# Two leftover token tiles of an attention + mixer kernel: from four plain half products to one pair in seven half products

## The chip, the cores and the metric

The kernel runs on one core of one Trainium2 chip. The metric is device time in microseconds. Before the change, three runs took 344.31, 344.91 and 345.24 us; their median, 344.91 us, is the time that the change is held against. A core has a matrix engine (TensorE, "PE" in the profile, with its weight loads "PEld"), VectorE ("DVE"), ScalarE ("ACT"), GpSimd ("POOL") and SyncE ("SP"); SP and ACT issue DMAs here, and 16 DMA engines move the data.

## What is computed

For each of 8 lots (batch entries) with 12 heads, 448 tokens and head width 64, the reference is, cut down:

```python
scores = q @ k.T / sqrt(64) - log(448)
x = (sigmoid(scores) @ v)                  # heads side by side: 448 tokens x 768
h = relu(x.T @ w_tok1) @ w_tok2            # mixes tokens, 448 -> 256 -> 448
u = x + h.T
out = u + relu(u @ w_ch1) @ w_ch2          # mixes channels, 768 -> 1536 -> 768
```

Only the last product, `relu(u @ w_ch1) @ w_ch2`, called the output stage here, is computed in another way by the change.

## The kernel before, in words

All matmuls are in float16 with float32 sums. The order of every engine's work is written out by hand; there is no scheduler, so the order of the Python calls is the order in which each engine's queue holds its instructions. Each engine runs its own queue in order and waits where an operand, or a buffer, is not ready.

The work is cut into 24 cycles, three per lot. A cycle does the scores of four heads (line 184, with the sigmoid on ACT, line 191), the product with the values of the cycle before (`av`, line 215), a transpose through DMA (`xtrans_dma`, line 240), and the token mixing of the cycle before that (`tok1`, line 293, with a relu on ACT, line 307; then `ytrans`, line 316, whose result DVE adds into `ut`, line 323). The channel mixing of a lot follows two cycles behind: `sevens` (line 499, called at the end of a lot) computes the hidden values `h2[lot]` as seven half-size products instead of eight, with sums of operands made beforehand; the outputs leave PSUM through ACT (lines 520, 522) and DVE (lines 529, 532). `utrans` (line 334, a DMA transpose issued by SP) gives `un`, the residual with tokens on partitions. `h2` has one buffer, so the next lot's `sevens` overwrites it.

The output stage takes `h2` (1536 hidden rows x 448 tokens) times `w_ch2` (`c2`). The 448 tokens are three tiles of 128 and a rest of 64. A plain half product (`ch2`, line 549) is 12 matmuls of 128 x 384 for one tile and one half of the 768 output columns, and one DVE addition of the residual (line 572). A whole tile is two of them, 24 matmuls. The rest of 64 tokens is `last_split` (line 631) for lot 6, and `ch2_last` (lines 802 and 813, evacuated by DVE and ACT at lines 825 and 823, stored at line 834) for lot 7.

For the last two lots a second way is used: the class `ch2_seven` takes two tiles at once. Two tiles, two halves of the hidden rows and two halves of the output columns form a 2 x 2 by 2 x 2 block product, which is done as seven products of six matmuls each (`plain`, line 763), 42 matmuls for two tiles. It needs four sums of hidden blocks, made by DVE (`sums`, line 751), and four sums of weight blocks (`hsums`, made once). The seven products run in three chains, X (products 1, 6, 7, 4), Y (2) and Z (5, 3). Each chain accumulates in one PSUM bank, and after each product DVE adds the bank as it stands into the output tile (`end`, line 781), so the next product of a chain can't start before that addition has read the bank. After products 3 and 4 a tile is whole, and `store` (line 585) has SP issue two DMAs of 64 rows.

The end of the program, from the last `av` on, is a sequence of its own, outside the loop. There are eight PSUM banks: four single ones called m0 to m3 (`at_bank` names the next), and two double ones under the tag "qk". In this end part lot 6 gives tiles 0 and 1 to `ch2_seven` and tile 2 to two plain half products; then `sevens` makes `h2` of lot 7; then lot 7 does the same: tiles 0 and 1 through `ch2_seven`, tile 2 as two plain half products (lines 1318 to 1332), the rest through `ch2_last`.

The core of the class before:

```python
def sums(self, first, last):
    for n, in0, in1, op in (
        (5, lambda: self.a21, lambda: self.a22, ADD),
        (6, lambda: s[5], lambda: self.a11, SUB),
        (7, lambda: self.a11, lambda: self.a21, SUB),
        (3, lambda: self.a12, lambda: s[6], SUB),
    )[first:last]:
        ...
```

Of the kernel before, what the change touches and what calls it, by code (L numbers as in the profile page):

```python
# [9 lines left out]
FP16 = mybir.dt.float16  # L10
# [13 lines left out]
NU = 3  # L24
# [6 lines left out]
def kernel(  # L31
# [53 lines left out]
    def bank(shape, dtype, name):  # L85

        if opening_banks:
            n = opening_banks.pop(0)
        else:
            n = at_bank[0]  # L90
            at_bank[0] = (n + 1) % 4
        return pp.tile(shape, dtype, tag=f"m{n}", bufs=1, name=name)
# [146 lines left out]
    def xtrans_dma(b, u):  # L239
        nc.sync.dma_start_transpose(  # L240
            out=xn_tile(b, u).rearrange("s g t d -> s (g t) d"),
            in_=xTs[b % 2][:, u, :, :].rearrange("d g s -> d (g s)"),
        )
# [38 lines left out]
    def tok1(b, u, relu_on_vector=False, with_scores=False):  # L282

        if not with_scores:
            h1_tile(b, u)
            one = bank([128, 2, 2, 128], FP32, f"tk_{b}_{u}")
            tks[b] = [one[:, tcb, :, :] for tcb in range(2)]
        ps = tks[b]
        for tcb in range(2):
            cols = slice(128 * tcb, 128 * tcb + 128)  # L290
            for t in range(3 if with_scores else 4):
                rows = slice(0, 64 if t == 3 and N_FIRST <= NU * b + u < N_CYCLES - 2 else 128)
                nc.tensor.matmul(  # L293
                    out=ps[tcb],
                    lhsT=w1[rows, t, cols],
                    rhs=xn[b, u][rows, :, t, :],
                    start=(t == 0 and not with_scores),
                    stop=(t == (2 if with_scores else 3)),
                )
        for tcb in range(2):  # L300
            dst, src = h1[b, u][:, tcb, :, :], ps[tcb]
            if relu_on_vector:
                nc.vector.tensor_scalar(
                    out=dst, in0=src, scalar1=0.0, scalar2=None, op0=MAX
                )
            else:
                nc.scalar.activation(out=dst, in_=src, func=RELU)  # L307

    def ytrans(b, u, banks=()):
        for g in range(2):  # L310
            db = NU * g + u
            if banks:
                at_bank[0] = banks[g]
            ps = bank([128, 512], FP32, f"yt_{b}_{db}")
            for tcb in range(2):
                nc.tensor.matmul(  # L316
                    out=ps[:, 0:S],
                    lhsT=h1[b, u][:, tcb, g, :],
                    rhs=w2[:, tcb, :, :],
                    start=(tcb == 0),  # L320
                    stop=(tcb == 1),
                )
            nc.vector.tensor_tensor(  # L323
                out=uts[b % 2][:, db, 0:S], in0=xTs[b % 2][:, u, g, 0:S], in1=ps[:, 0:S], op=ADD
            )


    def utrans(b):
        if b < B - 1:
            nc.vector.tensor_copy(  # L330
                out=uts[b % 2][:, 0:NU, S:512], in_=uts[b % 2][:, NU:NDB, S - 64 : S]
            )
        un[b] = pa.tile([128, NDB, 4, 128], FP16, tag="un", bufs=2, name=f"un_{b}")
        nc.sync.dma_start_transpose(
            out=un[b].rearrange("s db t d -> s (db t) d"),
            in_=uts[b % 2].rearrange("d db s -> d (db s)"),
        )
# [203 lines left out]
    def ch2(b, t, half, n0=0, n1=NCB):  # L541
        cols = slice(DH * half, DH * half + DH)
        if n0 == 0:
            if half == 0:
                outs[b, t] = pa.tile([128, D], FP32, tag="outs", bufs=3, name=f"o_{b}_{t}")
            acc[b] = bank([128, 512], FP32, f"c2_{b}_{t}_{half}")
        ps = acc[b]
        for cb in range(n0, n1):
            nc.tensor.matmul(  # L549
                out=ps[:, 0:DH],  # L550
                lhsT=h2[b][:, BY_GROUP[cb], 128 * t : 128 * t + 128],
                rhs=c2[:, BY_GROUP[cb], cols],
                start=(cb == 0),
                stop=(cb == NCB - 1 and b in un),
            )
        if n1 < NCB:
            return
        if b not in un:
            for n in range(NU):
                nc.tensor.matmul(  # L560
                    out=ps[:, 128 * n : 128 * n + 128],
                    lhsT=uts[b % 2][:, NU * half + n, 128 * t : 128 * t + 128],
                    rhs=ident[:, :],
                    start=False,
                    stop=(n == NU - 1),
                )
        ch2_out(b, t, half, ps)
# [147 lines left out]
    class ch2_seven:  # L715

        CHAIN = {1: "X", 6: "X", 7: "X", 4: "X", 2: "Y", 5: "Z", 3: "Z"}

        def __init__(self, b, X, Y, Z):
            self.b, self.ps, self.banks = b, {}, {"X": X, "Y": Y, "Z": Z}  # L720
            hid = pa.tile(
                [128, 3, NCB // 2, 128], FP16, tag="tr_k", bufs=2, name=f"hid_{b}"
            )
            hid3 = pa.tile([128, NCB // 2, 128], FP16, tag="tr_q", bufs=2, name=f"hid3_{b}")
            self.held = {n: hid[:, at, :, :] for at, n in enumerate((5, 6, 7))}
            self.held[3] = hid3[:, :, :]
            h = h2[b]
            t0, t1 = slice(0, 128), slice(128, 256)
            self.a11, self.a12 = h[:, LOW, t0], h[:, HIGH, t0]
            self.a21, self.a22 = h[:, LOW, t1], h[:, HIGH, t1]  # L730
            self.weights = {1: self.a11, 2: self.a12, 4: self.a22}
            self.moving = {
                1: c2[:, LOW, D1],
                2: c2[:, HIGH, D1],
                3: c2[:, HIGH, D2],
                5: hsums[0],
                6: hsums[1],
                7: hsums[2],
                4: hsums[3],
            }  # L740
# [12 lines left out]
        def begin(self, n):  # L753
            chain = self.CHAIN[n]
            if n in (1, 2, 5):
                at_bank[0] = self.banks[chain]
                self.ps[chain] = bank([128, 512], FP32, f"c8_{self.b}_{n}")
            return self.ps[chain]

        def plain(self, n, k0=0, k1=NCB // 2):  # L760
# [11 lines left out]
                self.end(n)  # L772

        def end(self, n):
            b = self.b
            t, half = {1: (0, 0), 2: (0, 0), 6: (0, 1), 3: (0, 1)}.get(n, (1, int(n != 4)))
            if (b, t) not in outs:
                outs[b, t] = pa.tile([128, D], FP32, tag="outs", bufs=3, name=f"o_{b}_{t}")
            o = outs[b, t][:, DH * half : DH * half + DH].rearrange("s (u d) -> s u d", d=128)
            opens = n in (1, 6, 5, 4)  # L780
            nc.vector.tensor_tensor(
                out=o,
                in0=un[b][:, NU * half : NU * half + NU, t, :] if opens else o,
                in1=self.ps[self.CHAIN[n]][:, 0:DH].rearrange("s (u d) -> s u d", d=128),
                op=ADD,
            )
            if n in (3, 4):
                store(b, t)
# [485 lines left out]

    lot = B - 2
    before, ahead = divmod(N_CYCLES - 1, NU), divmod(N_CYCLES - 2, NU)
    seven = ch2_seven(lot, X, X + 1, X + 1)
    av(*before, banks=two_banks("xa_end"))
    steps, last_end = last_split(lot, two_banks("c2_end"))
    for f in steps:  # L1280
        f()
    seven.sums(0, 2)

    def halves(b, t, half):
        return [lambda n=n: ch2(b, t, half, n, n + 6) for n in (0, 6)]

    first, second = halves(lot, 2, 0), halves(lot, 2, 1)
    xtrans_dma(*before)
    seven.plain(1)
    seven.plain(2)  # L1290
    seven.sums(2, 4)
    seven.plain(6)
    seven.plain(5)
    last_end()
    at_bank[0] = Y
    tok1(*ahead)
    seven.plain(7)
    seven.plain(3)
    at_bank[0] = Y
    ytrans(*ahead)  # L1300
    token_sums(B - 1, 0, 2)
    seven.plain(4)
    at_bank[0] = X + 1
    first[0]()
    at_bank[0] = Y
    tok1(*before)
    first[1]()
    at_bank[0] = Y
    ytrans(*before)
    at_bank[0] = X  # L1310
    second[0]()
    second[1]()
    token_sums(B - 1, 2, NU)
    utrans(B - 1)
    sevens(B - 1)
    seven = ch2_seven(B - 1, Y + 1, Y, X)
    first, second = halves(B - 1, 2, 0), halves(B - 1, 2, 1)
    seven.plain(1)
    seven.sums(0, 4)
    seven.plain(2)  # L1320
    at_bank[0] = X + 1
    for f in first:
        f()
    seven.plain(5)
    seven.plain(6)
    at_bank[0] = Y
    second[0]()
    seven.plain(3)
    seven.plain(7)
    second[1]()  # L1330
    seven.plain(4)
    at_bank[0] = X
    for w, f in pieces_last(B - 1):
        f()

# [29 lines left out]
```

## Time and profile before

| | value |
|---|---|
| runs | 344.31, 344.91, 345.24 us; median 344.91 us |
| the profiled execution's own time | 343.85 us |
| its span (first to last instruction) | 341.9 us |
| granted TensorE clock | 1.00 |
| busy: PE / PEld / DVE / ACT / POOL | 334.7 / 238.8 / 216.7 / 212.5 / 56.6 us |
| product of six 128 x 384 matmuls, start to start | 0.98 us |
| DVE addition of a 128 x 384 bank (lines 781, 572) | 0.55 to 0.56 us |
| DVE sum of hidden blocks, 128 x 768 f16 (line 751) | 0.49 to 0.56 us |
| ACT copy out of PSUM, 128 x 896 / 128 x 448 (lines 520, 522) | 0.92 / 0.54 us |
| lot 7's `sevens`, start | 312.36 us |
| lot 7's output stage, start / `ch2_last`, start | 324.43 / 335.25 us |
| the last two stores issued (ACT, SP) | 338.14 and 338.17 us |

Times in the trace are counted from the start of the span. "L763" is line 763 of the kernel before. A line of the timeline gives the start, the length, the engine, the line, the operation, what it writes and reads, and the number of instructions merged; in brackets stands the idle time before it and what ended it. "c" is any PSUM bank of the output stage, "hid" a sum of hidden blocks, "h" is `h2`, "o" an output tile, "hsum" a sum of weight blocks. A line of windows gives, for a stretch of time, each engine's busy time, the granted clock, the mean busy share of the DMA engines and the rate at which they moved data. SPq and ACTq are DMA-issuing instructions.

### The profile page before, as it was taken

How to read it: one execution, taken by the hardware profiler on the slowest of the kernel's cores; microseconds unless marked ns; L12 is line 12 of the kernel's file. 1: busy time of each engine (PE TensorE's matmuls, PEld its weight loads, DVE VectorE, ACT ScalarE, POOL GpSimd, SP SyncE). 2: the span in 40 equal slices, each digit the busy share in tenths (PEclk: the TensorE clock that was granted, in tenths of full speed). 3: DMA queues.
4: the chain of work that ended last, by engine and by line, in shares of the span. 5: the costliest groups of instructions: out<-in, count | busy, mean ns of one | idle time of the engine just before them, and what ended most of it. 6: DMA issues, size and time to landing. Idle time of an engine off the chain costs nothing.

```text
span 341.9 us, 10439 instructions
## 1 busy us (share of the span) xinstructions
PE 334.7 (98%) x4549; PEld 238.8 (70%) x4549; DVE 216.7 (63%) x438; ACT 212.5 (62%) x271; POOL 56.6 (17%) x98
## 2 busy tenths in 40 slices
PE   7999999999999999999999999999999999999994
PEld 4655566555886679766886679766896669768952
DVE  3376467588674775566574584666765685886662
ACT  4996846588658684877648785777648885102400
POOL 8992440040040004000130004000100000000000
PEclk9999999999999999999999999999999999999999
DMA  7999999999999799999999599948991438035406
GB/s 125 172 180 191 207 204 200 169 175 223 219 172 208 119 175 175 209 168 134 191 188 167 123 196 184 223 98 149 199 157 33 102 78 141 5 69 130 86 0 161
DMA packets 104380, 52.17 MB, mean 153 GB/s; under 512 B 76432, under 2 KB 101264, under 8 KB 104336
## 3 DMA queue, kind: packets, MB, share of 16 engines
q1 hardware_dynamic: 78944, 29.70, 47.8%
q0 software_dynamic: 25168, 21.50, 41.7%
q8 instruction: 35, 0.57, 0.7%
q10 hardware_dynamic: 224, 0.33, 0.3%
q14 instruction: 9, 0.07, 0.1%
HBM read 43.45 MB, written 11.01 MB: 159 GB/s over the span
## 4 chain that ended last, share of the span: by engine, by line
PE 90%; ACT 5%; DMA 1%; DVE 1%; issue 1%; ACTq 0%; DVEq 0%
PE c_ab L499 14%; PE qk L184 10%; PE c L549 9%; PE c_c L499 8%; PE c L375 8%; PE xa L215 8%; PE c L631 6%; PE tk L293 5%; PE yt L316 5%; ACT att L191 5%; PE c L763 4%; PE c L613 4%; PE c L352 3%; DMA first_q<-in_q_dram 1%; PE c L802 1%; PE c_a L499 1%
## 5 line engine op out<-in xcount | busy, mean ns | idle before, releaser
L191 ACT ACTIVATE att<-qk,att_bias 128x896 f16<-128x896 f32 x168 | 157.0, 1015 | 41.5 <-PE qk L184 41.1
L184 PE MATMUL qk<-tr_q,tr_k 64*64 64x448 f16 x672 | 57.5, 356 | 0.5 <-DVE tr_k L176 0.2
L499 PEld LDWEIGHTS <-c 128*128 128x128 f16 x504 | 48.4, 98 | 1.1 <-issue 0.3
L224 DVE CAST xT<-xa 128x448 f16<-128x448 f32 x46 | 26.6, 620 | 29.8 <-PE xa L215 29.8
L215 PE MATMUL xa<-att,raw_v 64*64 64x448 f16 x644 | 38.0, 349 | 0.0
L499 PEld LDWEIGHTS <-sum 128*128 128x128 f16 x378 | 36.3, 98 | 0.0
L184 PEld LDWEIGHTS <-tr_k 64*64 64x64 f16 x672 | 20.3, 105 | 19.7 <-issue 12.0
L572 DVE TENSOR_TENSOR o<-un,c 128x384 f32<-128x384 f16 x34 | 18.8, 554 | 23.3 <-PE c L613 10.2
L549 PE MATMUL c<-c,h 128*128 128x384 f16 x180 | 32.9, 326 | 0.0
L375 PE MATMUL c<-c,h 64*64 64x384 f16 x640 | 31.1, 322 | 0.0
L520 ACT ACTIVATE pt_ab<-c_ab 128x896 f32<-128x896 f32 x21 | 19.3, 917 | 16.9 <-PE c_ab L499 16.3
L323 DVE TENSOR_TENSOR ut<-xT,yt 128x448 f16<-128x448 f16 x48 | 27.5, 614 | 1.9 <-PE yt L316 1.9
L215 PEld LDWEIGHTS <-raw_v 64*64 64x64 f16 x672 | 20.3, 107 | 10.9 <-issue 0.4
L1039 POOL COPY gate<-tr_q 128x2 f16<-128x2 f16 x6 | 1.2, 195 | 154.0 <-DMA tr_q<-rel_q 154.0
L549 PEld LDWEIGHTS <-h 128*128 128x128 f16 x180 | 17.2, 98 | 11.3 <-issue 1.0
L307 ACT ACTIVATE h<-tk 128x256 f16<-128x256 f32 x42 | 14.2, 405 | 16.7 <-PE tk L293 16.7
L375 PEld LDWEIGHTS <-h 64*64 64x64 f16 x640 | 18.7, 107 | 7.9
L316 PE MATMUL yt<-w,h 128*128 128x448 f16 x96 | 22.1, 353 | 0.0
L631 PE MATMUL c<-c,h 64*64 64x384 f16 x480 | 22.1, 322 | 0.0
L522 ACT ACTIVATE h<-c_ab 128x896 f16<-128x896 f32 x7 | 6.4, 917 | 24.4 <-PE c_ab L499 24.4
L293 PE MATMUL tk<-xn,w 128*128 128x256 f16 x156 | 21.2, 274 | 0.1
L529 DVE TENSOR_TENSOR h<-pt_ab,c_ab 128x896 f16<-128x896 f32 x14 | 15.2, 1084 | 9.4 <-PE c_ab L499 9.4
(110 smaller groups left out, 473.3 us busy)
## 6 DMA issues: line engine op xcount, KB each, us to landing
out_dram<-o SPq DMA_DIRECT2D x48, 192.0 KB, 3.5
c<-in_moe_w_ch_dram POOLq DMA_DIRECT2D x4, 1152.0 KB, 15.6
raw_k<-in_k_dram POOLq DMA_DIRECT2D x10, 336.0 KB, 9.3
raw_q<-in_q_dram POOLq DMA_DIRECT2D x10, 336.0 KB, 13.3
raw_v<-in_v_dram POOLq DMA_DIRECT2D x10, 336.0 KB, 10.8
out_dram<-o SPq DMA_DIRECT2D x15, 96.0 KB, 2.2
raw_q<-in_q_dram POOLq DMA_DIRECT2D x12, 112.0 KB, 4.9
raw_k<-in_k_dram POOLq DMA_DIRECT2D x12, 112.0 KB, 4.8
```

The costliest lines, as they stand in the source:

```text
L184: nc.tensor.matmul(out=ps[64 * g : 64 * g + 64, hi, 0:S], lhsT=tr[b, "k"][64 * hi : 64 * hi + 64, u, j, 64 * g : 64 * g + 64], rhs=tr[b, " ...
L191: nc.scalar.activation(out=att[b, u, j][:, :, :], in_=ps[:, :, 0:S], func=SIGMOID, bias=bias_t[:, :], scale=att_scale,)
L215: nc.tensor.matmul(out=ps[g][64 * hi : 64 * hi + 64, 0:S], lhsT=raw[b, "v"][64 * g : 64 * g + 64, u, hi, j, :], rhs=att[b, u, j][64 * g : ...
L224: nc.vector.tensor_copy(out=xTs[b % 2][:, u, g, 0:S], in_=ps[g][:, 0:S])
L293: nc.tensor.matmul(out=ps[tcb], lhsT=w1[rows, t, cols], rhs=xn[b, u][rows, :, t, :], start=(t == 0 and not with_scores), stop=(t == (2 if ...
L316: nc.tensor.matmul(out=ps[:, 0:S], lhsT=h1[b, u][:, tcb, g, :], rhs=w2[:, tcb, :, :], start=(tcb == 0), stop=(tcb == 1),)
L323: nc.vector.tensor_tensor(out=uts[b % 2][:, db, 0:S], in0=xTs[b % 2][:, u, g, 0:S], in1=ps[:, 0:S], op=ADD)
L375: nc.tensor.matmul(out=ps[p][m : m + 64, 0:n], lhsT=lhsT(p, part, m), rhs=rhs(p, part), start=(first and turn == 0), stop=(last and turn = ...
L499: nc.tensor.matmul(out=ps[:, g, p, :], lhsT=weights[n][:, d, 128 * cb : 128 * cb + 128], rhs=moving[n][:, d, :], start=(n in (1, 5, 2) and ...
L520: nc.scalar.activation(out=shaped(part[:, :, :]), in_=ps, func=COPYF)
L549: nc.tensor.matmul(out=ps[:, 0:DH], lhsT=h2[b][:, BY_GROUP[cb], 128 * t : 128 * t + 128], rhs=c2[:, BY_GROUP[cb], cols], start=(cb == 0), ...
L631: nc.tensor.matmul(out=ps[r][m : m + 64, 0:DH], lhsT=lhsT(part, n, m), rhs=rhs(part, n, m), start=(n == 0), stop=(n == n_cb - 1),)
```

## The change

Tile 2 of lot 6 and tile 2 of lot 7 are now a pair of their own, and go through `ch2_seven` together after lot 7's `sevens`. Since `h2` is overwritten by then, ACT first copies lot 6's tile 2 (12 blocks of 128 tokens) to a tile `held`, in a buffer that the values of lot 6 have left. The output tile of lot 7's tile 2 takes another such buffer. The class gets the two rows of output and the two sides of hidden values as arguments. The order of the end is dealt anew: the token mixing and `utrans` of lot 7 stand earlier, between the products of lot 6's pair, `ytrans` writes to the double banks, `token_sums` is done in one piece instead of two, and the products of the two pairs of the last part alternate.

```diff
-    def ytrans(b, u, banks=()):
+    def ytrans(b, u, banks=None):
...
-            ps = bank([128, 512], FP32, f"yt_{b}_{db}")
+            ps = banks[g] if banks else bank([128, 512], FP32, f"yt_{b}_{db}")
...
-        def __init__(self, b, X, Y, Z):
+        def __init__(self, rows, sides, X, Y, Z):
...
+            (self.a11, self.a12), (self.a21, self.a22) = [
+                (side[:, LOW, :], side[:, HIGH, :]) for side in sides
+            ]
...
+    held = pa.tile([128, NCB, 128], FP16, tag="raw_v", bufs=2, name="held")
+    nc.scalar.activation(out=held[:, :, :], in_=tokens(h2[lot], 2), func=COPYF)
     seven.sums(0, 2)
-    first, second = halves(lot, 2, 0), halves(lot, 2, 1)
     xtrans_dma(*before)
+    last_end()
     seven.plain(1)
     seven.plain(2)
     seven.sums(2, 4)
-    seven.plain(6)
-    seven.plain(5)
-    last_end()
     at_bank[0] = Y
     tok1(*ahead)
+    seven.plain(6)
+    at_bank[0] = Y + 1
+    tok1(*before)
+    ytrans(*ahead, banks=two_banks("yt_end_1"))
+    seven.plain(5)
+    ytrans(*before, banks=two_banks("yt_end_2"))
+    utrans(B - 1)
     seven.plain(7)
+    token_sums(B - 1)
     seven.plain(3)
-    at_bank[0] = Y
-    ytrans(*ahead)
-    token_sums(B - 1, 0, 2)
     seven.plain(4)
-    first[0]()
-    tok1(*before)
-    first[1]()
-    ytrans(*before)
-    second[0]()
-    second[1]()
-    token_sums(B - 1, 2, NU)
-    utrans(B - 1)
     sevens(B - 1)
-    seven = ch2_seven(B - 1, Y + 1, Y, X)
-    first, second = halves(B - 1, 2, 0), halves(B - 1, 2, 1)
+    outs[B - 1, 2] = pa.tile([128, D], FP32, tag="raw_v", bufs=2, name=f"o_{B - 1}_2")
+    both = ch2_seven([(lot, 2), (B - 1, 2)], [held, tokens(h2[B - 1], 2)], Y, Y + 1, Y + 1)
+    seven = ch2_seven([(B - 1, 0), (B - 1, 1)], [...], X + 1, X, X)
+    both.plain(1)
+    seven.sums(0, 2)
+    both.plain(2)
     seven.plain(1)
-    seven.sums(0, 4)
     seven.plain(2)
-    for f in first:
-        f()
-    seven.plain(5)
+    both.sums(0, 2)
     seven.plain(6)
-    second[0]()
-    seven.plain(3)
+    seven.plain(5)
+    seven.sums(2, 4)
+    both.plain(6)
+    both.plain(5)
+    both.sums(2, 4)
     seven.plain(7)
-    second[1]()
+    seven.plain(3)
+    both.plain(7)
+    both.plain(3)
     seven.plain(4)
-    at_bank[0] = X
+    both.plain(4)
+    at_bank[0] = Y + 1
     for w, f in pieces_last(B - 1):
         f()
```

More of the change, by code (lines that the diff above doesn't have):

```diff
@@ L307, in tok1 @@
                 nc.scalar.activation(out=dst, in_=src, func=RELU)
-    def ytrans(b, u, banks=()):
+    def ytrans(b, u, banks=None):
         for g in range(2):
             db = NU * g + u
-            if banks:
-                at_bank[0] = banks[g]
-            ps = bank([128, 512], FP32, f"yt_{b}_{db}")
+            ps = banks[g] if banks else bank([128, 512], FP32, f"yt_{b}_{db}")
             for tcb in range(2):
@@ L717 @@
         CHAIN = {1: "X", 6: "X", 7: "X", 4: "X", 2: "Y", 5: "Z", 3: "Z"}
-        def __init__(self, b, X, Y, Z):
-            self.b, self.ps, self.banks = b, {}, {"X": X, "Y": Y, "Z": Z}
+        def __init__(self, rows, sides, X, Y, Z):
+            self.rows, self.ps, self.banks = rows, {}, {"X": X, "Y": Y, "Z": Z}
+            b = rows[1][0]
             hid = pa.tile(
@@ L726, in __init__ @@
             self.held[3] = hid3[:, :, :]
[L727 to L730, printed above, removed]
+            (self.a11, self.a12), (self.a21, self.a22) = [
+                (side[:, LOW, :], side[:, HIGH, :]) for side in sides
+            ]
             self.weights = {1: self.a11, 2: self.a12, 4: self.a22}
@@ L756, in begin @@
                 at_bank[0] = self.banks[chain]
-                self.ps[chain] = bank([128, 512], FP32, f"c8_{self.b}_{n}")
+                b, t = self.rows[1]
+                self.ps[chain] = bank([128, 512], FP32, f"c8_{b}_{t}_{n}")
             return self.ps[chain]
@@ L774, in end @@
         def end(self, n):
-            b = self.b
-            t, half = {1: (0, 0), 2: (0, 0), 6: (0, 1), 3: (0, 1)}.get(n, (1, int(n != 4)))
+            row, half = {1: (0, 0), 2: (0, 0), 6: (0, 1), 3: (0, 1)}.get(n, (1, int(n != 4)))
+            b, t = self.rows[row]
             if (b, t) not in outs:
@@ L1276, with tokens @@
     before, ahead = divmod(N_CYCLES - 1, NU), divmod(N_CYCLES - 2, NU)
-    seven = ch2_seven(lot, X, X + 1, X + 1)
+    def tokens(side, t):
+        return side[:, :, 128 * t : 128 * t + 128]
+    seven = ch2_seven(
+        [(lot, 0), (lot, 1)], [tokens(h2[lot], t) for t in range(2)], X, X + 1, X + 1
+    )
     av(*before, banks=two_banks("xa_end"))
@@ L1281 @@
         f()
+    held = pa.tile([128, NCB, 128], FP16, tag="raw_v", bufs=2, name="held")
+    nc.scalar.activation(out=held[:, :, :], in_=tokens(h2[lot], 2), func=COPYF)
     seven.sums(0, 2)
-    def halves(b, t, half):
-        return [lambda n=n: ch2(b, t, half, n, n + 6) for n in (0, 6)]
-    first, second = halves(lot, 2, 0), halves(lot, 2, 1)
     xtrans_dma(*before)
+    last_end()
     seven.plain(1)
@@ L1291 @@
     seven.sums(2, 4)
+    at_bank[0] = Y
+    tok1(*ahead)
+    seven.plain(6)
[5 more added lines that the diff above has]
+    utrans(B - 1)
+    seven.plain(7)
+    token_sums(B - 1)
+    seven.plain(3)
+    seven.plain(4)
+    sevens(B - 1)
+    outs[B - 1, 2] = pa.tile([128, D], FP32, tag="raw_v", bufs=2, name=f"o_{B - 1}_2")
+    both = ch2_seven(
+        [(lot, 2), (B - 1, 2)], [held, tokens(h2[B - 1], 2)], Y, Y + 1, Y + 1
+    )
+    seven = ch2_seven(
+        [(B - 1, 0), (B - 1, 1)], [tokens(h2[B - 1], t) for t in range(2)], X + 1, X, X
+    )
+    both.plain(1)
+    seven.sums(0, 2)
+    both.plain(2)
+    seven.plain(1)
+    seven.plain(2)
+    both.sums(0, 2)
     seven.plain(6)
     seven.plain(5)
-    last_end()
-    at_bank[0] = Y
-    tok1(*ahead)
+    seven.sums(2, 4)
+    both.plain(6)
+    both.plain(5)
+    both.sums(2, 4)
     seven.plain(7)
     seven.plain(3)
-    at_bank[0] = Y
-    ytrans(*ahead)
-    token_sums(B - 1, 0, 2)
+    both.plain(7)
+    both.plain(3)
     seven.plain(4)
-    at_bank[0] = X + 1
-    first[0]()
-    at_bank[0] = Y
-    tok1(*before)
-    first[1]()
-    at_bank[0] = Y
-    ytrans(*before)
-    at_bank[0] = X
-    second[0]()
-    second[1]()
-    token_sums(B - 1, 2, NU)
-    utrans(B - 1)
-    sevens(B - 1)
-    seven = ch2_seven(B - 1, Y + 1, Y, X)
-    first, second = halves(B - 1, 2, 0), halves(B - 1, 2, 1)
-    seven.plain(1)
-    seven.sums(0, 4)
-    seven.plain(2)
-    at_bank[0] = X + 1
-    for f in first:
-        f()
-    seven.plain(5)
-    seven.plain(6)
-    at_bank[0] = Y
-    second[0]()
-    seven.plain(3)
-    seven.plain(7)
-    second[1]()
-    seven.plain(4)
-    at_bank[0] = X
+    both.plain(4)
+    at_bank[0] = Y + 1
     for w, f in pieces_last(B - 1):
```

## The prediction

> **What bounds the kernel now.** I read the page's busy shares first, then the chain that ended last, then the end part alone: windows, the PE, DVE and SP timelines, and the DMA landings.
>
> ```profile
> PE 334.7 (98%) x4549; PEld 238.8 (70%) x4549; DVE 216.7 (63%) x438; ACT 212.5 (62%) x271; POOL 56.6 (17%) x98
> ...
> PE 90%; ACT 5%; DMA 1%; DVE 1%; issue 1%; ACTq 0%; DVEq 0%
> ```
>
> The reader is to see that 90% of the chain is PE. An average may hide a stage, so here are the windows of the output stage of lot 7:
>
> ```profile
> 325.00:330.00 5.00, 5.00 (x33) 2.99 (x32) 4.22 (x9) 0.17 (x1) 0.00 (x0) 1.00 0.00 0
> 330.00:335.00 5.00, 5.00 (x33) 2.99 (x31) 2.28 (x5) 0.00 (x0) 0.00 (x0) 1.00 0.18 37
> ```
>
> PE is busy 5.00 us of 5, at a clock of 1.00; DVE (third pair of numbers) is busy 4.22 us of 5 in the first half and is the engine to watch. The PE timeline gives the price of a product:
>
> ```profile
> 298.36 2.12 PE L763 MATMUL c<-c,h 128*128 128x384 f16 x12
> 300.32 2.11 PE L763 MATMUL c<-hsum,hid 128*128 128x384 f16 x12
> 302.27 1.04 PE L293 MATMUL tk<-xn,w 128*128 128x256 f16 x8
> 303.14 1.14 PE L763 MATMUL c<-hsum,hid 128*128 128x384 f16 x6
> ...
> 312.36 1.31 PE L499 MATMUL c_ab<-ut,c 128*128 128x224 f16 x12
> ...
> 324.43 2.11 PE L763 MATMUL c<-c,h 128*128 128x384 f16 x12
> ...
> 335.25 2.14 PE L802 MATMUL c<-c,h 128*64 128x384 f16 x24
> ```
>
> A length includes the tail of the last matmul, so I count from start to start: two products take 300.32 - 298.36 = 1.96 us, one 0.977, one matmul 0.163. No bracket with idle time stands on any PE line from 294 us on: matmuls removed there shorten the path one for one, as long as nothing else becomes late.
>
> **The change, part by part.**
>
> *Products.* Before, each tile 2 is two half products of 12 matmuls, 48 for both lots. After, the pair is 7 x 6 = 42. Six matmuls go: 6 x 0.163 = **0.98 us** off PE. Ahead of lot 7's `sevens` 24 matmuls leave (3.90 us), so it starts at 312.36 - 3.90 = 308.46; behind it 18 are added: 84 matmuls in place of 324.43 to 335.25's 66. Everything up to the end part is the same list of instructions.
>
> *The copy `held`.* ACT does 128 x 1536. No row has it; 0.54 us for 448 columns and 0.92 for 896 give 0.84 ns a column, so 1.46 us (between 0.92, the nearest row, and twice my value). It runs from 295.0, when `h2` is whole; ACT idles there for 8.5 us until 303.34, its next work comes at about 301.3, and `h2` is overwritten only after 308. Cost nothing; without that idle time it would delay the relu and then `ytrans` by its own length.
>
> *The token mixing, moved ahead.* The order is now products 1, 2, `tok1`, 6, `tok1` of the last cycle, `ytrans`, 5, `ytrans`, 7, 3, 4. The tightest need is the transposed xn for the second `tok1`: SP issues it at 297.82 as before, it landed 3.05 us later (300.87), and PE now wants it at 298.36 + 3 x 0.98 + 0.87 = 302.2 instead of 307.8. Slack 1.3 us: no cost. `last_end`'s additions come earlier on DVE, at 298.7, and delay product 1's addition from 299.55 to about 299.7 to 300.3; product 6 needs it at 301.2. SP's queue now has `last_end`'s stores and then `utrans` (about 306.7 instead of 314.3); the two stores of lot 6's pair wait behind its 4.3 us of issue, and nothing reads them. `token_sums` ends on DVE at 309.2, the first product that reads it comes at 311.3. Product 4 needs product 7's addition by 307.5; it ends at 307.27, the same 0.22 us of slack that product 6 had behind product 1 before (300.10 to 300.32), without a stall.
>
> *DVE in the last stage.* Before, the stage had 7 + 2 additions and 4 sums. After: 14 additions and 8 sums, 22 instructions in 13.7 us of PE. What one costs:
>
> ```profile
> 325.61 0.56 DVE L781 TENSOR_TENSOR o<-un,c 128x384 f32<-128x384 f16 x1 [0.31 <-PE c L763]
> 326.08 0.55 DVE L751 TENSOR_TENSOR hid<-h 128x768 f16<-128x768 f16 x1
> 326.66 0.56 DVE L751 TENSOR_TENSOR hid<-hid,h 128x768 f16<-128x768 f16 x1
> 327.14 0.55 DVE L751 TENSOR_TENSOR hid<-h 128x768 f16<-128x768 f16 x1
> ```
>
> Starts are 0.47 us apart, 0.58 where the second reads the first's result, and an addition starts 0.20 us after its product's last matmul was due to pass (325.41 to 325.61). I laid the new order out with these three numbers, keeping 324.43 as the stage's start. The pair's products 1 and 2 read `held` and cover the time in which `h2` is finished. Three places are tight. Product 6 of tiles 0 and 1 is due at 328.34; the addition before it in its bank ends at 328.16. Product 5 is due at 329.31; its bank is free at 329.09. Product 6 of the pair is due at 330.29; the sum that it loads as weights ends at 330.15 (it waits behind the addition of product 2 of tiles 0 and 1, 328.54). In the opening a weight load follows DVE by 0.10 us (xT copied by 29.39, load at 29.49), and the load itself takes 0.10: matmul at 330.35, a **stall of 0.06**. Bounds: 0 with no such delay, 0.30 if each instruction takes its full 0.56 and the delay is 0.20. All later needs have 0.2 us or more.
>
> *Stores at the end.* Four tiles leave in place of three in the last microseconds: tiles 0 of lot 7, 2 of lot 6, 1 and 2 of lot 7, the last three 0.98 us apart.
>
> ```profile
> 333.01 4.35 SPq L585 DMA_DIRECT2D out_dram<-o  x6
> ...
> 338.14 0.54 ACTq L834 DMA_DIRECT2D out_dram<-o  x1
> 338.17 0.47 SPq L834 DMA_DIRECT2D out_dram<-o  x1
> ```
>
> A tile takes SP two issues, 1.2 us. So three tiles ready at 333.0, 334.0 and 335.0 (before's clock less the 3.9 us) are issued until 336.7; the last store, due 0.92 us earlier than 338.17, at 337.25, finds SP free. The six landings before came 2.60, 2.70, 2.64, 2.75, 2.95 and 2.84 us after issue: two tiles in a row add 0.2 us, a third about 0.1 more. Before, the last pair of stores landed at 340.33 (SP, 2.16 us) and 340.56 (ACT, 2.42 us), 0.7 and 1.0 us behind the last tile's 339.60; now they come 0.3 us closer behind it. I take **0.10 us** lost, between 0 and 0.7 (the second rival).
>
> *The very end.* After the last landing SP steps through its final waits, a semaphore pair each:
>
> ```profile
> L1360 SPq EVENT_SEMAPHORE  x8: 27/28/28, 340.6 to 341.0; - x8
> L1360 SPq DRAIN  x1: 13/13/13, 341.1 to 341.1; - x1
> ```
>
> It waits for the eight DMA semaphores in a fixed order, 0.06 us a step. In before's instruction list ACT's last store, the latest to land (340.56), counts on the first of them, so eight steps follow it, 0.5 us to the drain at 341.07. In the changed list ACT's store has the last of the eight and SP's the third. SP's lands at 340.33 - 0.92 + 0.10 = 339.51; five steps later it is 339.82, ACT's has landed at 339.74, and the drain stands at about 339.90 instead of 341.07.
>
> *Sum.* PE's end: -0.98 + 0.06 = -0.92. Landing: +0.10. Final waits: 0.35 less. Together **-1.17 us**: a span of 341.9 - 1.2 = 340.7. The profiled execution took 343.85 us with a span of 341.9, so 1.95 lie around it; the median of the runs is 1.06 above it. I put the difference on the median: 344.91 - 1.17 = **343.75 us**, 0.34% less.
>
> **The rivals.**
>
> 1. *DVE becomes the bound of the last stage.* For: 22 instructions in 13.7 us, one each 0.62. Against: starts 0.47 to 0.58 apart in the same mix. At 0.60 apart PE would lose 0.7 us (344.4), at 0.65 1.5 us (345.2).
>
> 2. *The stores bunch up.* From the first data of lot 6's tile 2 to the end, three tiles and the last store are 1.38 MB. Two tiles in a row moved 0.79 MB from 336.0 to 339.3, 238 GB/s: 5.8 us from 334.3, to 340.1, where the forecast needs 339.4. That loses 0.7 us: 344.4. Against: the landings followed the issues by nearly the same time, so issue set that rate; at the 310 GB/s of 337 to 338 us nothing is lost. The Trainium skill ("Trainium Kernel Development and Optimization", Key Constraints) says that stores issued by SP and ACT run on the same 16 DMA engines and interleave, which speaks against the change: ACT's last store has no way past SP's tiles. The trace agrees in kind, 2.42 us on ACT beside 2.16 on SP. By its "Perfetto Trace Analysis" (Roofline), about 435 GB/s for one core, 1.38 MB would take an estimated 3.2 us and nothing would be lost.
>
> 3. *Slower: xn comes late.* The second `tok1` now reads xn 4.4 us after its transpose is issued, instead of 10. From a landing time of 4.4 us on PE waits one for one; from 5.6 us the kernel is slower than before. Lengths of 6.4 us (the median for tr_q) would cost 2.0 us: 345.8; the longest of this transpose was 11.3. Against: the last four took 3.0 to 3.2 us, with the DMA engines idle, as they are here (share 0.00 from 296 to 298 us).
>
> 4. *The end does not shorten*: the final waits cost what they did, because ACT's store lands well behind the rest, or the step order plays no part. -0.82 us: 344.1.
>
> **How the numbers follow.** Forecast 0.60, its own range 343.2 to 344.2 (stall 0 to 0.3, landing 0 to 0.3, and 0.4 us for the scatter of the runs). DVE bound 0.10, stores 0.10, xn late 0.05, end not shorter 0.12; 0.03 for a slowdown I have no row for. The range that holds 8 in 10 reaches down to 343.1 and up to **344.7**, over the second and fourth rival and the milder half of the first. 0.3% is 1.03 us, about what a measurement of this kernel can tell from no change, so faster means below 343.87. My forecast lies just beyond: of its 0.60 I give 0.50 to faster, with 0.05 from the others: 0.55. Slower (above 345.9) is half of the third rival, the far part of the first and the 0.03: 0.08. The rest, 0.37, is within 0.3%.
>
> **What would show it.** Lot 7's `sevens` starts at 308.5 in the new trace; `ch2_last` at about 334.3; PE has no idle bracket from 294 us on, or one of about 0.1 us at the pair's product 6. Then xn lands about 3 us after 297.8, and the copy `held` takes about 1.5 us on ACT ahead of 301. The last store is issued at 337.2, lands at 339.5 to 339.8, and the drain follows within 0.15 us of ACT's landing. Wrong would be: idle time of PE behind DVE in the last stage, the last store's landing over 2.7 us, or a `tok1` that waits for xn.

## The result, and the profile after

Over 21 runs of each kernel the median went from 344.93 to 345.9 us; the ratio is 1.0036 (95% interval 1.0019 to 1.0052). The change made the kernel slower by about a third of a per cent, where the prediction had 343.75 us and 343.1 to 344.7 as its range. The profiled execution of the changed kernel took 345.8 us with a span of 344.0, at a granted clock of 1.00.

Of the changed kernel's page, the busy shares and the chain that ended last by engine:

```profile
PE 335.3 (97%) x4543; PEld 238.7 (69%) x4543; DVE 219.6 (64%) x441; ACT 214.3 (62%) x272; POOL 56.7 (16%) x98
...
PE 90%; ACT 5%; DVE 2%; DMA 1%; issue 1%; ACTq 0%; DVEq 0%
```

PE has the six matmuls less (4543 for 4549), and still its busy time is 0.6 us longer and the chain gives DVE 2% where it gave 1%. By the windows of both traces the longer busy time lies ahead of lot 6's pair (296.76 us up to its first product, 295.46 before), where PE has the same instructions in both kernels; behind it PE is busy 38.55 us, 39.20 before. The last section treats that. What DVE has to do with the end shows in the chain from 303 us on. Its columns are start, length, and what was running:

```profile
304.40 0.39 PE yt_end L314 x2
...
304.81 0.63 DVE ut L321
...
305.49 0.54 PE yt_end L314 x2
...
307.04 0.56 DVE o L780
307.59 0.54 DVE ut L321
...
308.17 0.54 PE yt_end L314 x2
...
323.71 13.65 PE c L762 x84
```

Twice the chain leaves PE for DVE in the middle of a `ytrans`: two matmuls, an addition on DVE, then the other two matmuls. The PE timeline of the same stretch says how long PE stood still:

```profile
304.23 0.54 PE L314 MATMUL yt_end<-w,h 128*128 128x448 f16 x2
305.49 0.54 PE L314 MATMUL yt_end<-w,h 128*128 128x448 f16 x2 [0.71 <-DVE ut L321]
305.86 1.14 PE L762 MATMUL c<-hsum,hid 128*128 128x384 f16 x6
306.84 0.54 PE L314 MATMUL yt_end<-w,h 128*128 128x448 f16 x2
308.17 0.54 PE L314 MATMUL yt_end<-w,h 128*128 128x448 f16 x2 [0.80 <-DVE ut L321]
308.55 1.14 PE L762 MATMUL c<-hsum,hid 128*128 128x384 f16 x6
...
311.47 1.31 PE L497 MATMUL c_ab<-ut,c 128*128 128x224 f16 x12
...
323.55 2.11 PE L762 MATMUL c<-c,held 128*128 128x384 f16 x12
...
337.29 2.14 PE L801 MATMUL c<-c,h 128*64 128x384 f16 x24
```

The two brackets are waits that the prediction does not have. From start to start the two halves of a `ytrans` are 1.26 us (305.49 - 304.23) and 1.33 us (308.17 - 306.84) apart; without a wait they are 0.38 (two matmuls of 448 columns, as e1 below shows). 1.26 + 1.33 - 2 x 0.38 = **1.83 us** lost. The 84 matmuls of the last stage, from 323.71 on, have no gap.

**One clock for two traces.** Up to product 1 of lot 6's pair (298.36 us before, 299.55 after) PE has the same instructions in both kernels, yet the after trace is 1.19 us late there. That belongs to the execution (the last section shows from what). So I measure all kernels from this product's start, which takes the scatter of the opening out: to lot 7's `sevens`, to `ch2_last`, and to the end of the span.

| kernel | `sevens` | `ch2_last` | end | last two stores, issue to landing (ACT / SP) | last landing to end | median, us | ratio to before [95%] |
|---|---|---|---|---|---|---|---|
| before | 14.00 | 36.89 | 43.55 | 2.42 / 2.16 | 1.35 | 344.93 | |
| after | 11.92 | 37.74 | 44.48 | 2.79 / 2.59 | 1.05 | 345.9 | 1.0036 [1.0019, 1.0052] |
| e1_own_tiles | 10.09 | 35.91 | 42.66 | 2.83 / 2.62 | 1.03 | 344.31 | 0.9978 [0.9960, 0.9997] |
| e2_pair_early | 10.10 | 35.91 | 42.68 | 2.52 / 2.27 | 1.35 | 343.92 | 0.9954 [0.9941, 0.9968] |
| e3_pair_alone | 11.00 | 36.93 | 43.68 | 2.82 / 2.62 | 1.03 | 345.0 | 0.9993 [0.9976, 1.0010] |
| e4_one_store_less | 10.10 | 35.91 | 42.33 | 2.42 / 2.15 | 1.11 | 343.51 | 0.9949 [0.9921, 0.9978] |
| e5_stores_on_two_queues | 10.09 | 35.91 | 42.50 | 2.42 / 2.15 | 1.28 | 344.04 | 0.9995 [0.9967, 1.0023] |
| e6_products_then_adds | 10.09 | 35.91 | 42.65 | 2.81 / 2.61 | 1.05 | 344.01 | 0.9973 [0.9951, 0.9994] |
| e7_reorder_alone | 14.00 | 36.89 | 43.60 | 2.47 / 2.20 | 1.35 | 344.73 | 1.0009 [0.9992, 1.0025] |
| e8_last_wait_last | 10.09 | 35.91 | 42.32 | 2.41 / 2.14 | 1.11 | 343.68 | 0.9968 [0.9949, 0.9986] |

The kernel before, run beside e1 to e4, had a median of 345.14; beside e5 to e8, 345.05.

From this mark the change costs 44.48 - 43.55 = +0.93 us; the medians differ by 0.97. Its parts: products -0.98 (24 matmuls less ahead of `sevens`, -3.90, and 18 more behind it, 25.82 us from `sevens` to `ch2_last` in place of 22.89: +2.93; a rounding of 0.01), the waits in `ytrans` +1.83, the landing of ACT's last store +0.37, the final waits -0.30. Together +0.92.

### The profile page after: what moved, and what is told of

Its sections match the earlier page's. It is cut to its first block, busy times and chain, and to the rows that moved or that the text cites. A ratio compares the mean times of both kernels' runs of the same rounds, so it can differ in the third digit from the quotient of the medians.

```text
span 344.0 us, 10437 instructions
## 1 busy us (share of the span) xinstructions
PE 335.3 (97%) x4543; PEld 238.7 (69%) x4543; DVE 219.6 (64%) x441; ACT 214.3 (62%) x272; POOL 56.7 (16%) x98
## 4 chain that ended last, share of the span: by engine, by line
PE 90%; ACT 5%; DVE 2%; DMA 1%; issue 1%; ACTq 0%; DVEq 0%
PE c_ab L497 14%; PE qk L184 10%; PE c_c L497 8%; PE c L373 8%; PE xa L215 8%; PE c L547 6%; PE c L762 6%; PE c L629 6%; PE tk L293 5%; PE yt L314 5%; ACT att L191 5%; PE c L611 4%; PE c L350 3%; DMA first_q<-in_q_dram 1%; PE c L801 1%; PE c_a L497 1%
## 5 line engine op out<-in xcount | busy, mean ns | idle before, releaser
L570 DVE TENSOR_TENSOR o<-un,c 128x384 f32<-128x384 f16 x30 | 16.6, 554 | 20.7 <-PE c L611 10.2
L321 DVE TENSOR_TENSOR ut<-xT,yt 128x448 f16<-128x448 f16 x44 | 25.2, 615 | 1.9 <-PE yt L314 1.9
L373 PEld LDWEIGHTS <-h 64*64 64x64 f16 x640 | 18.7, 107 | 7.9
L547 PE MATMUL c<-c,h 128*128 128x384 f16 x132 | 24.1, 326 | 0.0
L527 DVE TENSOR_TENSOR h<-pt_c,c_c 128x448 f16<-128x448 f32 x21 | 13.0, 617 | 12.3 <-PE c_c L497 12.3
L314 PE MATMUL yt<-w,h 128*128 128x448 f16 x88 | 20.3, 353 | 0.0
L629 PEld LDWEIGHTS <-h 64*64 64x64 f16 x528 | 15.4, 107 | 6.7
```

The lines of the kernel that those rows point to most:

```text
L314: nc.tensor.matmul(out=ps[:, 0:S], lhsT=h1[b, u][:, tcb, g, :], rhs=w2[:, tcb, :, :], start=(tcb == 0), stop=(tcb == 1),)
L321: nc.vector.tensor_tensor(out=uts[b % 2][:, db, 0:S], in0=xTs[b % 2][:, u, g, 0:S], in1=ps[:, 0:S], op=ADD)
L373: nc.tensor.matmul(out=ps[p][m : m + 64, 0:n], lhsT=lhsT(p, part, m), rhs=rhs(p, part), start=(first and turn == 0), stop=(last and turn = ...
L527: nc.vector.tensor_tensor(out=shaped(dst), in0=shaped(parts[gs, which]), in1=ps, op=ADD)
L547: nc.tensor.matmul(out=ps[:, 0:DH], lhsT=h2[b][:, BY_GROUP[cb], 128 * t : 128 * t + 128], rhs=c2[:, BY_GROUP[cb], cols], start=(cb == 0), ...
L629: nc.tensor.matmul(out=ps[r][m : m + 64, 0:DH], lhsT=lhsT(part, n, m), rhs=rhs(part, n, m), start=(n == 0), stop=(n == n_cb - 1),)
```

## The experiments

My theory after the result: `ytrans` gets both halves of a double bank as one tile. The code writes half 0, has DVE add it, writes half 1, has DVE add that. Waits are kept by tile, so the second product waits until the first addition has read the tile, though it writes another bank. The changed kernel's instruction list for PE has that wait (a row is the number, the line, the instruction, and what it waits for):

```
8564 L314 Matmult yt_end_5994<-w_69,h_7_2_5966 128x448
...
8568 L314 Matmult yt_end_5994<-w_69,h_7_2_5966 128x448 [waits DVE_49]
```

The rivals were that the token mixing's relu comes late in the new order, and that the loss is only the opening's scatter. The second is out by the table: the loss stands behind the mark, +0.93 us, and the medians of 21 runs each agree with it.

**e1_own_tiles**: each product gets a tile, and with it a double bank, of its own.

```diff
-    ytrans(*ahead, banks=two_banks("yt_end_1"))
+    ytrans(*ahead, banks=[two_banks(f"yt_end_1{g}")[0] for g in range(2)])
(yt_end_2 likewise)
```

> The changed kernel, with each of the four ytrans products of the last lot in a double bank of its own (its first half used) instead of two products sharing one double bank as one tile. Theory T (one tile, one wait): the second product of each pair waits until DVE has read the first, because both lie in one tile; in the trace of the changed kernel this is 1.26 us from start to start instead of 0.38, and 1.33 instead of 0.38, together 1.83 us. T expects both gaps at 0.38, sevens of lot 7 starting 10.1 us after product 1 of lot 6's pair (11.92 in the changed kernel, 14.0 in the kernel before), and a time 1.8 us below the changed kernel, near 344.1 us, 0.25% below the kernel before. Rival R1 (the relu is late: tok1 now stands close ahead of ytrans): the gaps stay, 345.9 us. Rival R2 (the loss is the 1.19 us by which the opening of the profiled execution was longer, all else is even): no change, 345.9 us, with the opening 1.2 us longer than in the kernel before.

PE's timeline of e1:

```profile
305.76 0.92 PE L314 MATMUL yt_end<-w,h 128*128 128x448 f16 x4
306.52 1.14 PE L762 MATMUL c<-hsum,hid 128*128 128x384 f16 x6
307.50 0.92 PE L314 MATMUL yt_end<-w,h 128*128 128x448 f16 x4
```

Both brackets are gone: four matmuls in 0.76 us (306.52 - 305.76), and the end comes 44.48 - 42.66 = 1.82 us sooner, the 1.83 of the two waits. With that alone the change pays, if narrowly: 0.9978, with an interval that ends at 0.9997.

**e6_products_then_adds**: the tile stays shared; in `ytrans` both products are written before the two additions.

```diff
-            nc.vector.tensor_tensor(out=uts[b % 2][:, db, 0:S], ..., in1=ps[:, 0:S], op=ADD)
+            adds.append(add)        # add holds this same addition
+            if not banks:
+                adds.pop()()
+        for add in adds:
+            add()
```

> The changed kernel with its shared double banks kept, but in each ytrans both products are written first and DVE's two additions come after them, as av does with its two banks. Theory T: the second product then has no reader ahead of it in its tile, PE does not wait, sevens of lot 7 starts 10.1 us after product 1 of lot 6's pair, time as e1, near 344.2 us. R1 (late relu): 11.9 us and 345.9 us.

PE's timeline of e6 at the two `ytrans`, and DVE's at the first:

```profile
304.82 0.92 PE L315 MATMUL yt_end<-w,h 128*128 128x448 f16 x4
...
306.55 0.92 PE L315 MATMUL yt_end<-w,h 128*128 128x448 f16 x4
```

```profile
305.77 1.15 DVE L324 TENSOR_TENSOR ut<-xT,yt_end 128x448 f16<-128x448 f16 x2 [1.07 <-PE yt_end L315]
```

Same tile, same banks, no wait on PE: the order of writers and readers was what cost the time. DVE shows the tile as the unit from the other side. Its first addition starts 0.95 us after the products' start, 0.2 after all four matmuls (304.82 + 0.76). In e1, with a tile each, it starts at 306.34, 0.58 after 305.76, 0.2 after the first two (0.38). The chip itself does not ask for it: by the Trainium skill ("PSUM — Partial Sum Buffer", section "PSUM bank collisions raise a hardware error") two engines must be kept apart on one bank, and these are two banks. The runs agree so far as e1, in which the products have no order to the other's addition, takes the full 1.82 us back.

**e3_pair_alone**: the pair in the last part as in after, but the order ahead of lot 7's `sevens` as before.

```diff
+    last_end(); tok1(*ahead)      # behind product 5, ahead of 7
+    ytrans(*ahead)                # behind product 3, single banks
+    tok1(*before); ytrans(*before); utrans(B - 1)   # behind product 4
```

> The pair in seven products alone: tok1, ytrans, token_sums and utrans of lot 7 stay where they were in the kernel before, in single banks; only the plain half products of lot 6's tile 2 that stood between them are gone. Theory T: no wait on a shared tile, but the relu of the second tok1 has nothing to hide behind: PE idles about 0.95 us ahead of the second ytrans and about 0.2 at the start of sevens. Time: 344.9 - 0.98 + 1.15 + 0.4 (stores) - 0.3 (final waits) = 345.2 us, 0.7 below the changed kernel. R1 and R2: no better than the changed kernel, 345.9 or above.

PE's timeline of e3, ahead of `sevens`:

```profile
309.97 0.92 PE L314 MATMUL yt<-w,h 128*128 128x448 f16 x4 [0.75 <-ACT h L307]
310.72 1.42 PE L497 MATMUL c_ab<-ut,c 128*128 128x224 f16 x12
```

This is what the first rival looks like: PE waits 0.75 us for the relu (ACT, line 307), because the plain halves of tile 2 that covered it are gone. `sevens` starts 0.91 later than in e1, and the last store still lands late. From the mark the end is 43.68, 0.13 behind before; timed, 0.9993. So by the traces the pair needs the reordered front to gain anything (43.68 here, 42.66 in e1; the intervals of the timed ratios overlap), and e1 and e6, which have it, show no wait for the relu at all. The rival falls for after.

**e7_reorder_alone**: e1's front, but without `held` and the second pair; tile 2 of both lots in plain halves as before.

```diff
-    held = pa.tile([128, NCB, 128], FP16, tag="raw_v", bufs=2, name="held")
-    nc.scalar.activation(out=held[:, :, :], in_=tokens(h2[lot], 2), func=COPYF)
...
+    for f in halves(lot, 2, 0) + halves(lot, 2, 1):
+        f()
```

> The new order of the token mixing alone, with own tiles for ytrans as in e1, but without the pair: tile 2 of lot 6 and of lot 7 go through plain half products as in the kernel before (lot 6's four groups stand together ahead of sevens). As many matmuls as before, no wait: sevens 14.0 us after product 1, the span's end 43.55 us after it, time that of the kernel before, 344.9 to 345.2 us, ratio 1.000. If the new order itself cost something that the pair hides, it shows here as idle time of PE.

Every mark is that of before within 0.05 us, and the ratio is 1.0009. Moving the token mixing costs nothing and brings nothing by itself.

**e4_one_store_less**: e1 without the store of lot 6's tile 2.

```diff
-            if n in (3, 4):
+            if n in (3, 4) and (b, t) != (B - 2, 2):
                 store(b, t)
```

> e1_own_tiles without the two DMAs that store lot 6's tile 2 (that tile of the output is left unwritten). T: with one tile less in the last microseconds the last two stores land 2.4 us (ACT) and 2.2 us (SP) after issue, as in the kernel before; in this list ACT's store has the seventh of the eight final waits, SP's the first. Time 0.4 us below e1, near 343.7 us. If it is not the number of stores that delays the last ones, the lags stay at 2.6 to 2.8 us and the time at that of e1.

The time from issue to landing of the last two stores (SP, ACT), after and e4:

```profile
DMA to landing us min/median/max: 2.6/2.7/2.8
```

```profile
DMA to landing us min/median/max: 2.1/2.3/2.4
```

One tile less in front of them, and they are as quick as before the change; the end comes 0.33 us sooner than in e1. So the stores in front are what makes them late. It need not be the number of tiles: e4 also has two tiles in a row where after has three (1.20 and 1.28 us apart), and its last tile store is issued 1.37 us ahead of ACT's last store, after's 1.07. In e2 below all four tiles are stored, but in rows of two and with the same 1.37 us, and most of the delay is gone. The runs do not separate the row from that distance. In after the eight tile stores land 2.61, 2.71, 2.62, 2.73, 2.98, 2.94, 2.94 and 3.06 us after their issue.

**e2_pair_early**: e1, with the last stage dealt so that the pair's tiles leave earlier and further apart; the sums move along with their products.

```diff
-    (1, 2 of both; 1, 2 of seven; 6, 5, 6, 5, 7, 3, 7, 3, 4, 4 alternating)
+    both 1, 2; seven 1, 2; both 6, 5, 7, 3; seven 6; both 4; seven 5, 7, 3, 4
```

> e1_own_tiles, and in the last stage the products of the pair of tiles 2 are drawn ahead, so that the tiles are whole 1.95, 2.9 and 0.98 us apart instead of three of them 0.98 us apart, as many products as before. Theory T adds that three tiles stored 0.98 us apart hold up the last two stores (2.79 us on ACT and 2.59 on SP after issue in the changed kernel, 2.42 and 2.16 before): here they should fall back to about 2.4 and 2.2, 0.4 us less. In this kernel's list ACT's last store counts on the first of the eight DMA semaphores that SP waits for at the end, as in the kernel before, so about 0.35 us after the last landing come back: together 344.0 us, as e1 or 0.1 below. If the stores are not held up by each other, the lags stay at 2.6 to 2.8 and the time is 0.35 above e1.

The stores do land sooner (2.52 and 2.27), but the span ends as in e1: ACT's store, the last to land, now counts on the first of the eight final waits, so 1.35 us follow it, not 1.03. The gain of 0.31 in landing was given back there. Its timed ratio, 0.9954 from five runs, is better than the trace accounts for (-0.87 us, or 0.9975).

**e5_stores_on_two_queues**: e2, with the second half of each of the last tiles issued by ACT.

```diff
-            nc.sync.dma_start(
+            queue = nc.scalar if par == 1 and (b == B - 1 or (b, t) == (B - 2, 2)) else nc.sync
+            queue.dma_start(
```

> e2_pair_early, and the second half of each of the last four tiles is issued by ACT instead of SP. The stores stand in time 0.6 us less behind each other at issue. T: the last two stores land 2.4 (ACT) and 2.2 us (SP) after issue as in the kernel before (2.52 and 2.27 in e2): from the start of product 1 of lot 6's pair to the end 42.6 us (42.68 in e2), time 0.1 below e2, near 343.8 us. ACT's last store counts on the second of the eight final waits. If ACT's issues get in the way of its last copy, the last store is issued later than SP's by over 0.3 us and the time is above e2.

The last stores land as in e4, with all tiles stored, and the span ends 0.16 us sooner than e1's. The timed ratio, 0.9995 with an interval 0.56% wide, cannot tell that: three of twelve runs were above 346 us.

**e8_last_wait_last**: e5, and two earlier stores go through GpSimd's queue, so that ACT's last store counts on the last of the final waits.

```diff
+            if (b, t) == (B - 2, 0):
+                queue = nc.gpsimd
```

> e5_stores_on_two_queues, and the two DMAs of lot 6's tile 0, some 25 us before the end, are issued by GpSimd. They are off every path; what they change is the count of DMAs, so that ACT's last store counts on the eighth and SP's on the first of the eight semaphores that SP waits for at the end. If the order of the final waits is worth what the traces show (1.35 us from the last landing to the end of the span where ACT's store counts on the first, 1.05 where it counts on the last), the time is 0.3 us below e5, near 343.5 us, and 1.05 us lie between the last landing and the end. If the order plays no part, both are as in e5, with 1.3 us.

1.11 us follow the last landing instead of 1.28: 0.18 us less at the end, not 0.3, because in e5 the store had come to stand on the second wait. It is not 1.05 either: SP's last store now counts on the first wait and lands at 340.42, and the steps run on from 340.43 to 340.89, so that the last of them finds ACT's store, landed at 340.65, already there. In e4, with SP's store on the first wait and ACT's on the seventh, 1.11 us follow as well. By the trace e8 ends 1.23 us ahead of before; timed it is 0.9968. Of the versions tried it has the shortest end with all stores in place, and it is faster than both kernels; e2's and e8's intervals overlap, so the runs do not tell which of the two is the faster.

## Why the prediction was wrong, point by point

- *Products*: right. Without the waits `sevens` comes 3.91 us sooner (10.09 for 14.00; forecast 3.90), and the 18 matmuls behind it cost 2.93.
- *The copy `held`*: right. It took 1.48 us (estimate 1.46), from 296.20, in ACT's idle time.
- *The token mixing, moved ahead, "no cost"*: **this step failed, by 1.83 us.** It followed each operand (xn landed 3.04 us after its issue, 1.3 us ahead of its use, as forecast; the relu was in time) and each chain's bank, but of `ytrans` only its place. That both its products now lie in one tile, with a DVE addition between them in the code, was in the diff (`banks[g]` from one `two_banks`). Before, each product took a tile of its own from m0 and m1. The second wait is longer than the first because DVE does product 5's addition (307.04) first and only then the addition that PE waits for (307.51), as DVE's timeline of after shows. The 0.03 that I gave to "a slowdown I have no row for" was the place of this case, and 0.08 for slower was too little.

```profile
307.04 0.56 DVE L780 TENSOR_TENSOR o<-un,c 128x384 f32<-128x384 f16 x1 [0.35 <-PE c L762]
307.51 0.61 DVE L321 TENSOR_TENSOR ut<-xT,yt_end 128x448 f16<-128x448 f16 x1
```

- *DVE in the last stage*: no stall, where I had 0.06. At the pair's product 6, its sum ended at 329.26, when it was due by the forecast (330.15 on before's clock, less 0.88), but the weight load followed at 329.32, 0.05 us later where I had taken 0.10, and the matmul started in its turn at 329.40. DVE's share in that stage, after:

```profile
325.00:330.00 5.00, 5.00 (x33) 3.02 (x31) 4.55 (x10) 0.00 (x0) 0.00 (x0) 1.00 0.00 0
330.00:335.00 5.00, 5.00 (x33) 3.01 (x31) 4.58 (x10) 0.00 (x0) 0.00 (x0) 1.00 0.00 0
```

  DVE is busy 4.55 and 4.58 us of 5, PE all 5.00. The first rival falls, with little room. How 0.60 and 0.65 us for one instruction come to 0.7 and 1.5 us the prediction does not show (22 x 0.60 = 13.2 us is less than the stage's 13.7), and no run tests these two prices.
- *Stores at the end*: the mechanism was right, the term mis-sized: +0.37 for 0.10, within its bounds of 0 to 0.7. I read the lags of two tiles in a row and added 0.1 for a third; the last two stores lost 0.37 and 0.43. The second rival is thus half true, as e4 and e2 show.
- *The very end*: right. After the last landing 1.05 us follow, 1.35 before: -0.30 for -0.35. Five steps are left behind SP's landing at 342.80, with ACT's at 342.98. The final waits of after:

```profile
L1362 SPq EVENT_SEMAPHORE  x5: 28/28/28, 342.9 to 343.1; - x5
L1362 SPq DRAIN  x2: 7/10/13, 343.2 to 343.3; - x2
```

- *Third rival, xn late*: fell; no `tok1` waits. *Fourth rival*: fell; in e2, where ACT's store counts on the first of the waits again, 1.35 us follow again.
- *The base*: putting the difference on the median, not on the profiled time, was right; before's profiled execution had a quick opening, with the earliest start of the common mark of the ten traces (298.36 us).

With the wait taken away the forecast's sum is nearly met: -0.89 us by the trace of e1 for -1.17. The 0.28 between them are 0.31 in the stores' landing (+0.41 in e1 for 0.10) and 0.03 in the final waits (-0.32 for -0.35), less the stall of 0.06 that did not come. e8 reaches -1.23.

## What to carry to other kernels

In this program two banks handed out as one tile are one tile for the waits: product, reader, product, reader on it makes PE wait for each reader, so write all products first or give each its own tile; and when a step moves to other buffers, look in the instruction list for the waits it gained, even if all its operands are early. At the end of a program the last store counts three times, by what is stored ahead of it, by its queue, and by the place of its semaphore, and of the store's that lands just ahead of it, in the final waits. Where a change is worth less than the scatter of the opening, compare traces from a common mark and not by their spans.

## What the runs showed of the hardware

The same instructions of the opening took different times from one execution to another. Before, then after, PE's timeline at 5.8 us:

```profile
5.79 0.58 PE L167 MATMUL tp_q<-ident,raw_q 128*64 128x128 f16 x14 [1.13 <-DVE raw_q L953]
```

```profile
5.79 0.96 PE L167 MATMUL tp_q<-ident,raw_q 128*64 128x128 f16 x14 [1.14 <-DVE raw_q L952]
```

The 14 transposes start at the same time and take 0.58 or 0.96 us. The matmuls behind them are slower too, such as three of the warm-up tile `heat`, before and after:

```profile
6.41 0.50 PE L940 MATMUL heat<-warm 128*128 128x256 f16 x3
```

```profile
6.90 0.82 PE L939 MATMUL heat<-warm 128*128 128x256 f16 x3
```

At 12 us the after trace is 1.20 us behind, which is all of the 1.19. The cause is the granted clock. Each trace keeps records of it, and the first of them, at full clock, starts at 5.05 us before and at 9.40 us after. Ahead of it matmuls of `heat` follow each other 213 ns apart, behind it 109 ns. The profile's page counts the time ahead of the first record as full, so its row of granted clocks shows 9 in every slice of both, and the 1.00 given for the whole span does not hold for the opening. The full clock began at 4.3 to 5.1 us in before, e4, e6 and e7, and at 9.4 to 10.3 us in after, e1, e2, e3, e5 and e8, which share the same opening, so it is no matter of the change. The Trainium skill ("TensorE: Matmul & The Clock Gate", "Part 1: The HAM clock gate (the "warmup" mystery)") describes such a thing: PE runs at half speed until a free-running window of activity has been seen busy, and how many matmuls that hits differs from run to run, for under 1% of a span. The traces agree in kind (213 / 109 = 1.95) and in size (1.2 of 344 us, 0.35%), but that is as much as the whole effect of this change. Why the full clock came late in one execution and not in another, no run here shows.

The start of the common mark lay anywhere from 298.36 to 301.08 us. Beside the clock, PE's waits for DMAs made the difference: for the first weight block at about 33 us (0.82 us in e4, 1.73 in e6, 0.22 in e7), and for a transposed xn (1.25 us in e1 at 117.72 us, 1.00 in e2 at 77.28). So the wait that the prediction's third rival describes does occur in this program; but the last transpose, which the rival is about, landed 3.04 to 3.06 us after its issue in all ten traces.
